# Queries of head pairs by seven block products in place of eight

## The chip, the cores and the metric

The kernel runs on one core of a Trainium2 chip. The metric is the device time of one execution in microseconds; less is better. TensorE (PE) multiplies, VectorE (DVE) and ScalarE (ACT) work elementwise, GpSimd (POOL) has a few statistics at the start, and SyncE (SP) issues nearly all DMAs.

## The reference

A layer norm feeds an attention block with cached keys and values (32 heads, 2048 queries, 2048 keys, head width 128) and a gated mixer (two residual blocks). The mixer's result, through SiLU, multiplies the attention's.

```python
xn = _layernorm(x)                                   # x: 2048 x 512
q = (xn @ wq).reshape(1, 2048, 32, 128)              # wq: 512 x 4096
p = softmax(einsum("bhqd,bhkd->bhqk", q, k_cache) * 128**-0.5)
s = einsum("bhqk,bhkd->bhqd", p, v_cache) @ wo       # wo: 4096 x 512
g = silu(mixer(xn, w1, w2, w3, w4))
return x + s * g
```

The change concerns `xn @ wq`.

## The kernel before, in words

After some 120 us of layer norms and mixer, the kernel walks through 128 *units*. A unit is one head with 512 queries: 8 groups of 4 heads, in each group 4 query quarters (`qt`), in each the 4 heads (`hh`). `HG` = 4, `NG` = 8, `QT` = 4, `NU` = 128, `SPU` = 8.

A unit has 8 *slots* (`p` = 0 to 7; `n` = 8 u + p counts them through). In each slot PE makes the scores of 256 keys (`s_slot`: two matmuls 128x512 into one of two score buffers) and the values of the slot ten before (`pv_run`: two matmuls 128x512). ACT takes the exponential of the scores, 128x1024, into `pT`. Beside that, most slots hold one more matmul, a filler: in slots 7, 0, 1, 2 the queries of the next unit (`q_mm`, four contraction chunks of 128, into `ps_q`, tag `xa`, one buffer), in slots 3 to 6 one token tile of the output projection (`wo_slot`, four heads, into `ps_wo`, tag `xm`, one buffer).

DVE does, in each unit and in this order: `turned_sums` of the unit before last (L383, L385), `add_next` (L345), `fold` (L349), `fold_last` (L353), `q_copy` of the next unit's queries (L318), `add_first` (L340), `add_next` (L345), `wo_post` (L467; more in the last groups), `norm` (L403). L340 and L345 add `pT` tiles into `acc` and wait for ACT. The row sums are turned by a DMA (`tT`), inverted, written out (`dr`) and read back to all partitions (`rb`), and `norm` multiplies the values with them.

In the last groups `wo_post` has more to do. In units 95 to 110 one `y_scale` (L433) or `y_add` (L438) comes in a unit, placed by `at`. For the later two query quarters of group 6 (posts in units 110 to 117) it is L460 and L463. For the first two quarters of group 7 (posts in units 118 to 125) it is L467, L476 and L478 and the output's DMA.

Every engine issues its instructions in the program's order. `pin` keeps the order in which the Python code emits them; `at(n, fn)` puts work at the end of slot n. A pool with n buffers makes the n+1st tile wait until the first is free. The last unit is cut into two token halves by hand-written code behind the loop.

Of the kernel before, what the change touches and what calls it, by code (L numbers as in the profile page):

```python
# [9 lines left out]
ALU = mybir.AluOpType  # L10
# [7 lines left out]
def kernel(  # L18
# [15 lines left out]
    nc = tc.nc  # L34
# [72 lines left out]
    w2_v = B_w2.rearrange("(dc p) j -> p dc j", p=P)  # L107
    w3_v = B_w3.rearrange("(dc p) f -> p dc f", p=P)

    def mm(out, lhsT, rhs, start, stop):  # L110
        pin(nc.tensor.matmul(out=out, lhsT=lhsT, rhs=rhs, start=start, stop=stop))  # L111

    pin(nc.vector.memset(warm[:], 0.0))
    pin(nc.vector.memset(ones_t[:], 1.0))
# [48 lines left out]
    vX = {}  # L163
    xin = {}

    def load_x(t, eng):
        xin[t] = tokp.tile([P, D], BF16, tag="ta", bufs=10, name="xin")
        pin(eng.dma_start(out=xin[t][:], in_=xsrc[t]))

    def load_pair(t, eng):  # L170
# [99 lines left out]
    def ln2(t):  # L270
        c, ts = divmod(t, 4)
        if ts == 0:
            xn2T[c] = pL.tile([P, DC, 512], BF16, tag="xn2T", bufs=2, name="xn2T")
        y = tokp.tile([P, D], BF16, tag="ta", bufs=10, name="xn2")
# [19 lines left out]
        pin(nc.vector.tensor_tensor(out=xall[:, t, :], in0=ps[:], in1=xall[:, t, :], op=ALU.add))  # L294

    def gate_tanh(t):
        th = tokp.tile([P, D], BF16, tag="ta", bufs=10, name="th")
        pin(nc.scalar.activation(out=th[:], in_=xall[:, t, :], func=ACT.Tanh, scale=0.5))
        return th

# [6 lines left out]
    def q_mm(u, dcs, tag="xa"):  # L307
        g, qt, hh = units[u]
        if dcs[0] == 0:
            st[u] = dict(psq=psX.tile([P, 512], FP32, tag=tag, name="ps_q"))  # L310
        for dc in dcs:
            mm(st[u]["psq"][:], wqs[g * HG + hh][:, dc, :],
               xnT[:, dc, qt * 512:(qt + 1) * 512], dc == 0, dc == DC - 1)

    def q_copy(u, eng=None):
        qT = qtp.tile([P, 512], BF16, name="qT")
        if eng is None:
            pin(nc.vector.tensor_copy(out=qT[:], in_=st[u].pop("psq")[:]))  # L318
        else:
            pin(nc.scalar.activation(out=qT[:], in_=st[u].pop("psq")[:], func=ACT.Identity))  # L320
        st[u]["qT"] = qT

    def s_slot(u, p):
        g, qt, hh = units[u]
# [126 lines left out]
    def wo_post(g, t, n):  # L451
        ps = wo_box.pop(0)
        if g == 0:
            sacc[t] = pS.tile([P, D], FP32, tag="sacc", bufs=NT, name="sacc")
            pin(nc.vector.tensor_copy(out=sacc[t][:], in_=ps[:]))
            return
        sa, gl = sacc[t][:], xall[:, t, :]
        if t // 4 in LATE and g >= GY:
            tm = pS.tile([P, D], FP32, tag="tm", bufs=4, name="tm")
            pin(nc.vector.scalar_tensor_tensor(  # L460
                out=tm[:], in0=ps[:], scalar=0.5, in1=gl, op0=ALU.mult, op1=ALU.mult))
            if g < NG - 1:
# [4 lines left out]
        pin(nc.vector.tensor_tensor(out=sa, in0=ps[:], in1=sa, op=ALU.add))  # L467
# [8 lines left out]
        pin(nc.vector.scalar_tensor_tensor(  # L476
            out=gl, in0=sa, scalar=0.5, in1=gl, op0=ALU.mult, op1=ALU.mult))
        pin(nc.vector.tensor_tensor(out=xl[:], in0=gl, in1=xl[:], op=ALU.add))  # L478
        pin(nc.sync.dma_start(out=out2d[t * P:(t + 1) * P, :], in_=xl[:]))
# [57 lines left out]
                   hh == 0, hh == HG - 1 and (ts in apart or c.stop == D))  # L537

    def last_act(ts, cols):
        tb[ts, cols.start] = tokp.tile([P, D // 2], BF16, tag="ta", bufs=10, name="tb")  # L540
# [241 lines left out]
    def wo_slot(part, n, each=2, **kw):  # L782
# [9 lines left out]
    q_plan = defaultdict(list)  # L792
    for v in range(1, NU):
        if v not in made:
            for dc in range(DC):
                q_plan[(v - 1) * SPU + dc - 1].append((v, (dc,)))

    for n in range(UB * SPU):
        u, p = divmod(n, SPU)
# [4 lines left out]
        pv_run(n)  # L804
        for v, dcs in q_plan.get(n, ()):
            q_mm(v, dcs)
        if p == 0 and u - 2 in TURN:
            turned_sums(u - 2)
        if p == 1 and u - 2 in TURN:
# [9 lines left out]
            twice = extra  # L819
        if twice and p < 3:  # L820
            wo_slot(p, n, tag="xa")
        if p == 3 and u + 1 not in made:
            q_copy(u + 1)
# [14 lines left out]
        if wo_p <= p <= wo_p + HG // each and wo_todo and pS is not None and (p == wo_p or wo_box):  # L838
            wo_slot(p - wo_p, n, each=each)
        if p == norm_p and u - 2 in TURN:  # L840
            norm_queue(u - 2)
        if p == 4:
            add_first(u)
        if p == 6:
# [19 lines left out]

    def last_stt(ts, cols):
        w = cols.stop - cols.start
        tb[ts, cols.start] = pS.tile([P, w], FP32, tag="tm", bufs=4, name="tm")
        pin(nc.vector.scalar_tensor_tensor(  # L868
            out=tb[ts, cols.start][:], in0=last_ps(ts, cols), scalar=0.5, in1=xall[:, t0 + ts, cols],
            op0=ALU.mult, op1=ALU.mult))  # L870

    def last_add(ts, cols, tm):
        if cols.start == 0:
            yl[ts] = tokp.tile([P, D], BF16, tag="ta", bufs=10, name="y")
        pin(nc.vector.tensor_tensor(out=yl[ts][:, cols], in0=tm, in1=sacc[t0 + ts][:, cols], op=ALU.add))  # L875

    def last_out(ts, cols, queue=nc.sync):
# [135 lines left out]
```

## Time and profile before

| | |
|---|---|
| median of 3 runs | 1243.86 us (1243.78 to 1243.9) |
| span of the profiled execution, first to last instruction | 1242.0 us |
| granted TensorE clock, mean | 1.000 |
| PE busy | 1231.2 us |
| ACT busy | 1110.7 us |
| DVE busy | 1006.7 us |
| mean of a 128x512 query copy (L318) | 683 ns |

The profiled execution's own time is its span; the runs' times lie 1.86 us above it by their median. In rows of a timeline stand the start, the time from start to shown end, engine, line, operation, output and inputs with shapes, how many in a row, and in brackets the idle time ahead with what ended it. A matmul's shown end lies behind the end of its stream, so that consecutive matmuls overlap in the rows; the rate is read from the starts. In a row of stretches come, after the window and its length, the busy time of PE, PEld (weight loads), DVE, ACT and POOL with their counts, then the granted clock, the share of DMA and GB/s.

### The profile page before, as it was taken

To read this page: it belongs to the slowest core of one execution; us is meant where nothing else is said; L and a number is where in the kernel's file an instruction comes from. 1 tells how busy PE (TensorE), PEld (TensorE's weight loads), DVE (VectorE), ACT (ScalarE), POOL (GpSimd) and SP (SyncE) were. 2 spreads that over 40 slices of the span, in tenths; PEclk is the share of its full clock that TensorE was granted. 3 is DMA by queue.
4 is the path that set the end of the run, shared out by engine and by line. 5 is a ranking of instruction groups with operands and counts; after the bars stand their busy time and mean duration, and the time that the engine had idled before them with its cause. 6 is when DMAs were issued, how large, how long until landed. Compare 5 with 4: busy or idle time off the path is not lost.

```text
span 1242.0 us, 16355 instructions
## 1 busy us (share of the span) xinstructions
PE 1231.2 (99%) x5822; PEld 613.6 (49%) x5937; DVE 1006.7 (81%) x1465; ACT 1110.7 (89%) x1127; POOL 26.6 (2%) x75
## 2 busy tenths in 40 slices
PE   9999999999999999999999999999999999999998
PEld 6444444444444444444444444444444444444445
DVE  7712778888888888888888888888888988999997
ACT  6345999999999999999999999999999999999996
POOL 5200000000000000000000000000000000000000
PEclk9999999999999999999999999999999999999999
DMA  7660113553335513453244423543346424552332
GB/s 180 165 141 29 30 39 75 92 110 73 68 80 104 111 40 85 89 112 77 56 103 90 103 53 72 104 104 69 73 85 113 101 60 89 99 109 63 77 79 66
DMA packets 244050, 107.67 MB, mean 87 GB/s; under 512 B 194816, under 2 KB 227712, under 8 KB 243968
## 3 DMA queue, kind: packets, MB, share of 16 engines
q1 hardware_dynamic: 243408, 106.17, 40.7%
q8 instruction: 46, 0.75, 0.3%
q10 hardware_dynamic: 560, 0.46, 0.1%
q14 instruction: 36, 0.29, 0.1%
HBM read 67.50 MB, written 2.36 MB: 56 GB/s over the span
## 4 chain that ended last, share of the span: by engine, by line
PE 98%; issue 1%; DMA 0%; DVE 0%; ACT 0%; POOL 0%; DVEq 0%
PE ps_s L111 42%; PE ps_o L111 38%; PE ps_q L111 8%; PE ps_wo L111 8%; PE ps_m L111 2%; DMA xin<-in_A_x_dram 0%; PE ps_oh L111 0%; DVE y L875 0%; DMA out_dram<-y 0%; DVE tm L868 0%; DVE tb L546 0%; ACT dump L202 0%; POOL rs L186 0%; PE ps_w L111 0%; DVE xall L217 0%
## 5 line engine op out<-in xcount | busy, mean ns | idle before, releaser
L334 ACT ACTIVATE pT<-ps_s 128x1024 bf16<-128x1024 f32 x1016 | 1038.1, 1024 | 59.4 <-PE ps_s L111 6.5
L111 PE MATMUL ps_s<-qT,kT 128*128 128x512 bf16 (+1 forms) x2061 | 608.5, 377 | 5.1
L111 PE MATMUL ps_o<-pT,vb 128*128 128x512 bf16 x1980 | 589.0, 379 | 0.2
L345 DVE TENSOR_TENSOR acc<-acc,pT 128x2048 bf16<-128x2048 bf16 x254 | 307.4, 1210 | 104.7 <-ACT pT L334 104.6
L111 PEld LDWEIGHTS <-kT 128*128 128x128 bf16 x2064 | 233.7, 113 | 217.7
L111 PEld LDWEIGHTS <-vb 128*128 128x128 bf16 x1984 | 194.0, 98 | 217.0
L340 DVE TENSOR_TENSOR acc<-pT 128x2048 bf16<-128x2048 bf16 x127 | 155.2, 1222 | 39.9 <-ACT pT L334 39.8
L111 PE MATMUL ps_wo<-wo_h,oT 128*128 128x512 bf16 x448 | 168.3, 379 | 0.1
L111 PE MATMUL ps_q<-xnT,wq_h 128*128 128x512 bf16 x458 | 167.4, 379 | 0.2
L349 DVE TENSOR_TENSOR acc<-acc 128x1024 bf16<-128x1024 bf16 x127 | 87.8, 691 | 4.3
L111 PEld LDWEIGHTS <-oT 128*128 128x128 bf16 x528 | 59.4, 113 | 57.8
L403 DVE TENSOR_TENSOR oT<-ps_o,rb 128x512 bf16<-128x512 f32 x127 | 86.6, 682 | 0.9 <-DMA rb<-dr 0.6
L383 DVE TENSOR_REDUCE sm<-tT 128x4 f32<-128x512 bf16 x124 | 83.9, 676 | 0.4 <-DMA tT<-acc 0.4
L318 DVE CAST qT<-ps_q 128x512 bf16<-128x512 f32 x116 | 79.3, 683 | 0.0
L111 PEld LDWEIGHTS <-wq_h 128*128 128x128 bf16 x508 | 49.7, 98 | 59.3
L467 DVE TENSOR_TENSOR sacc<-ps_wo,sacc 128x512 f32<-128x512 f32 x96 | 65.6, 683 | 0.0
L353 DVE TENSOR_TENSOR acc<-acc 128x512 bf16<-128x512 bf16 x127 | 54.1, 426 | 4.3
L285 ACT ACTIVATE h2T<-ps_s 128x1024 bf16<-128x1024 f32 x28 | 28.7, 1024 | 26.0 <-PE ps_s L111 25.3
L111 PE MATMUL ps_s<-xn2T,w_sb 128*128 128x512 bf16 x220 | 48.6, 379 | 0.2
L111 PEld LDWEIGHTS <-w_sb 128*128 128x128 bf16 x368 | 33.6, 98 | 29.6
L111 PEld LDWEIGHTS <-h2T 128*128 128x128 bf16 x224 | 21.9, 98 | 26.3
L294 DVE TENSOR_TENSOR xall<-ps_o,xall 128x512 bf16<-128x512 f32 x8 | 5.5, 692 | 36.0 <-PE ps_o L111 36.0
(86 smaller groups left out, 361.7 us busy)
## 6 DMA issues: line engine op xcount, KB each, us to landing
rb<-dr SPq DMA_DIRECT2D x127, 256.0 KB, 3.9
vb<-in_A_v_cache_dram SPq DMA_DIRECT2D x62, 256.0 KB, 3.0
wq_h<-in_A_wq_dram SPq DMA_DIRECT2D x32, 128.0 KB, 3.3
wo_h<-in_A_wo_dram SPq DMA_DIRECT2D x32, 128.0 KB, 3.0
w_sb<-in_B_w_dram SPq DMA_DIRECT2D x8, 256.0 KB, 4.8
kT<-in_A_k_cache_dram SPq DMA_TRANSPOSE x128, 2.8
xl<-in_A_x_dram SPq DMA_DIRECT2D x16, 128.0 KB, 3.2
dr<-rc SPq DMA_DIRECT2D x127, 2.0 KB, 1.4
```

Of the source, the lines that this page charges most:

```text
L111: pin(nc.tensor.matmul(out=out, lhsT=lhsT, rhs=rhs, start=start, stop=stop))
L285: pin(nc.scalar.activation(out=h2[c, f][:], in_=ps[:], func=ACT.Gelu_apprx_tanh))
L294: pin(nc.vector.tensor_tensor(out=xall[:, t, :], in0=ps[:], in1=xall[:, t, :], op=ALU.add))
L318: pin(nc.vector.tensor_copy(out=qT[:], in_=st[u].pop("psq")[:]))
L334: pin(nc.scalar.activation(out=s["pT"][-1][:, jj:jj + 2, :], in_=sps[:], func=ACT.Exp, scale=SCALE))
L340: pin(nc.vector.tensor_tensor(out=s["acc"][:], in0=s["pT"][0][:], in1=s["pT"][1][:], op=ALU.add))
L345: pin(nc.vector.tensor_tensor(out=a[:], in0=a[:], in1=st[u]["pT"][i][:], op=ALU.add))
L349: pin(nc.vector.tensor_tensor(out=a[:, 0:2, :], in0=a[:, 0:2, :], in1=a[:, 2:4, :], op=ALU.add))
L353: pin(nc.vector.tensor_tensor(out=a[:, 0, :], in0=a[:, 0, :], in1=a[:, 1, :], op=ALU.add))
L383: pin(nc.vector.tensor_reduce(out=sm[:], in_=s["tT"][:], axis=mybir.AxisListType.X, op=ALU.add))
L403: pin(nc.vector.tensor_tensor(out=to, in0=o, in1=rb, op=ALU.mult))
L467: pin(nc.vector.tensor_tensor(out=sa, in0=ps[:], in1=sa, op=ALU.add))
```

## The change

For 57 pairs of heads (units 12 to 125) the queries of two neighbouring heads and one query quarter are made together. The product has 512 tokens, 512 contraction rows and 2 x 128 output columns. It is cut in two along each: token halves, contraction halves, the two heads. Instead of eight block products, seven are formed from sums of blocks (the scheme of Strassen in Winograd's form). A block product is two matmuls 128x256, so a pair has 14 of them, where two units had eight of 128x512.

The sums of token blocks (`x_sum`, four for each query quarter, bf16, 128x512) and of weight blocks (`w_sum`, four for each pair of heads, bf16, 128x256) are made once, on DVE. The sums of products are made partly by PE, which adds two products in one half of a bank, and partly by DVE (`q_part`, four parts a pair, here q0 to q3) on the way from PSUM to the queries. Both halves, `ps[:, 0]` and `ps[:, 1]`, are one bank of tag `xa`.

For the pair (v, v+1), v even, everything happens two units ahead: products 1, 6, 2 in slots 1, 2, 5 of unit v-2 (the *even* unit), 7, 5, 4, 3 in slots 0, 1, 4, 5 of unit v-1 (the *odd* unit); q0 at slot 3 and q1 at slot 6 of the even unit, q2 at slot 3 and q3 at slot 6 of the odd one. On DVE q0 and q2 take the place of `q_copy`, ahead of `add_first`; q1 and q3 stand between `add_first` and `add_next`. q0 reads both halves (two operations), q1 copies one, q2 reads both (two operations, the second depends on the first), q3 is one operation of 128x512. The output projection's matmuls go to other slots (`at_wo`): 0, 3, 4, 6 or 3, 4, 5, 6 in even units, 0, 2, 3, 6 in odd ones, its post still at slot 7. The slots of a pair then hold 15 fillers instead of 16. The queries of unit 11 move four slots ahead, to slots 3 to 6 of unit 9.

To make room, small token tiles get other pools (`token`), the last head's values take a buffer of the common pool, early queries lie in the right-hand pool, and `tm` has two buffers. Behind the changed lines the numbers shift: `mm` is on L112, `q_part` on L388 to L400, `add_first` L422, `add_next` L427, `wo_post` L549, `norm` L485.

```diff
-    qtp = ent(pool("qt", 3 * HG + 2))
+    qtp = ent(pool("qt", 6))
+    qp2 = ent(pool("qp2", 2))
...
+    def x_sum(qt, i):
+        if i == 2 and qt < QT - 1:
+            out = x_block(qt, 1, LO)
+        else:
+            out = pS.tile([P, 2, 256], BF16, tag="xs", bufs=XS, name="xs")[:]
+        a, b, op = (
+            (x_block(qt, 1, LO), x_block(qt, 1, HI), ALU.add),
+            (xs.get((qt, 0)), x_block(qt, 0, LO), ALU.subtract),
+            (x_block(qt, 0, LO), x_block(qt, 1, LO), ALU.subtract),
+            (x_block(qt, 0, HI), xs.get((qt, 1)), ALU.subtract),
+        )[i]
+        pin(nc.vector.tensor_tensor(out=out, in0=a, in1=b, op=op))
+        xs[qt, i] = out
+
+    def w_sum(h, i):
+        if i == 0:
+            wc[h] = pS.tile([P, 4, 2, Dh], BF16, tag="wc", bufs=2, name="wc")
+        w, o = wc[h], [wc[h][:, k] for k in range(4)]
+        b11, b12, b21, b22 = (wqs[h + j][:, d, :] for d in (LO, HI) for j in (0, 1))
+        a, b = ((b12, b11), (b22, o[0]), (b22, b12), (b21, o[1]))[i]
+        pin(nc.vector.tensor_tensor(out=o[i], in0=a, in1=b, op=ALU.subtract))
+
+    def product(v, k):
...
+        if k in (1, 7):
+            s["ps"] = psX.tile([P, 2, 256], FP32, tag="xa", name="ps_q")
...
+        side, x, b = {
+            1: (0, x_block(qt, 0, LO), b11),
+            2: (0, x_block(qt, 0, HI), b21),
+            3: (1, xs[qt, 3], b22),
+            4: (0, x_block(qt, 1, HI), o[3]),
+            5: (1, xs[qt, 0], o[0]),
+            6: (1, xs[qt, 1], o[1]),
+            7: (0, xs[qt, 2], o[2]),
+        }[k]
+        for dc in range(2):
+            mm(s["ps"][:, side, :], b[:, dc, :], x[:, dc, :], k in (1, 7) and dc == 0, True, skip_group_check=True)
+
+    def q_part(v, i):
+        s = sw[v]
+        ps, t = s["ps"], lambda: pS.tile([P, 256], FP32, tag="tq", bufs=3, name="tq")
+        if i == 0:
+            m1, s["u"] = t(), t()
+            pin(nc.vector.tensor_copy(out=m1[:], in_=ps[:, 0, :]))
+            pin(nc.vector.tensor_tensor(out=s["u"][:], in0=ps[:, 1, :], in1=m1[:], op=ALU.add))
+        elif i == 1:
+            q = s["q"] = qp2.tile([P, 4, 256], BF16, name="qT")
+            pin(nc.vector.tensor_copy(out=q[:, 0, :], in_=ps[:, 0, :]))
...
+        elif i == 2:
+            u3 = t()
+            pin(nc.vector.tensor_tensor(out=u3[:], in0=ps[:, 0, :], in1=s["u"][:], op=ALU.add))
+            pin(nc.vector.tensor_tensor(out=s["q"][:, 3, :], in0=ps[:, 1, :], in1=u3[:], op=ALU.add))
+        else:
+            pin(nc.vector.tensor_tensor(
+                out=s["q"][:, 1:3, :], in0=ps[:], in1=s["u"][:].unsqueeze(1).to_broadcast([P, 2, 256]),
+                op=ALU.add))
...
-            tm = pS.tile([P, D], FP32, tag="tm", bufs=4, name="tm")
+            tm = pS.tile([P, D], FP32, tag="tm", bufs=2, name="tm")
...
+    FIRST, LAST = 12, NU - 4
+    pairs = range(FIRST, LAST + 1, 2)
     q_plan = defaultdict(list)
+    steps = defaultdict(list)
+    for v in pairs:
+        a = (v - 2) * SPU
+        for k, n in ((1, 1), (6, 2), (2, 5), (7, 8), (5, 9), (4, 12), (3, 13)):
+            steps[a + n].append((product, v, k))
+        for i, n in enumerate((3, 6, 11, 14)):
+            steps[a + n].append((q_part, v, i))
...
+    for qt, u in ((QT - 1, 8), (0, 10), (1, 14), (2, 18)):
+        for i in range(4):
+            at((u + i // 2) * SPU + 1 + 4 * (i % 2), lambda qt=qt, i=i: x_sum(qt, i))
+    for h in range(0, H, 2):
+        u = (h // HG) * QT * HG + (-4, -2)[h % HG // 2]
+        for i in range(4):
+            n = max(u, 8) * SPU if h < HG else (u + i // 2) * SPU
+            at(n + (2, 6)[i % 2] + (i // 2) * (h < HG) + 8 * (h % HG == 2) * (h < HG), lambda h=h, i=i: w_sum(h, i))
+
     for v in range(1, NU):
-        if v not in made:
+        if v not in made and not FIRST <= v < LAST + 2:
             for dc in range(DC):
-                q_plan[(v - 1) * SPU + dc - 1].append((v, (dc,)))
+                q_plan[(v - 1) * SPU + dc - 1 if v > FIRST else (v - 2) * SPU + dc + 3].append((v, (dc,)))
...
+        at_wo = [wo_p + i for i in range(HG // each + 1)]
+        if FIRST - 2 <= u < LAST:
+            at_wo = ([0, 3, 4, 6, 7], [0, 2, 3, 6, 7], [3, 4, 5, 6, 7], [0, 2, 3, 6, 7])[u % 4]
```

More of the change, by code (lines that the diff above doesn't have):

```diff
@@ L164, with token @@
     xin = {}
+    def token(early, name):
+        if early:
+            return pL.tile([P, D], BF16, tag="xi", bufs=5, name=name)
+        return tokp.tile([P, D], BF16, tag="ta", bufs=6, name=name)
     def load_x(t, eng):
-        xin[t] = tokp.tile([P, D], BF16, tag="ta", bufs=10, name="xin")
+        xin[t] = token(t < 5, "xin")
         pin(eng.dma_start(out=xin[t][:], in_=xsrc[t]))
@@ L321, in q_copy, with x_block @@
         st[u]["qT"] = qT
+    xs = {}
+    wc = {}
+    sw = {}
+    LO, HI = slice(0, 2), slice(2, 4)
+    def x_block(qt, half, dcs):
+        c = qt * 512 + 256 * half
+        return xnT[:, dcs, c:c + 256]
+    def x_sum(qt, i):
[11 more added lines that the diff above has]
+        xs[qt, i] = out
@@ new lines, in w_sum @@
+    def w_sum(h, i):
[6 more added lines that the diff above has]
+    def product(v, k):
+        g, qt, hh = units[v]
+        h = g * HG + hh
+        s = sw.setdefault(v, {})
+        if k in (1, 7):
+            s["ps"] = psX.tile([P, 2, 256], FP32, tag="xa", name="ps_q")
+        w, o = wc[h], [wc[h][:, i] for i in range(4)]
+        b11, _, b21, b22 = (wqs[h + j][:, d, :] for d in (LO, HI) for j in (0, 1))
+        side, x, b = {
[9 more added lines that the diff above has]
+            mm(s["ps"][:, side, :], b[:, dc, :], x[:, dc, :], k in (1, 7) and dc == 0, True, skip_group_check=True)
@@ new lines, in q_part @@
+    def q_part(v, i):
[8 more added lines that the diff above has]
+            pin(nc.vector.tensor_copy(out=q[:, 0, :], in_=ps[:, 0, :]))
+            for j in range(2):
+                st[v + j] = dict(qT=q[:, 2 * j:2 * j + 2, :].rearrange("d a b -> d (a b)"))
+        elif i == 2:
[6 more added lines that the diff above has]
+                op=ALU.add))
+            del sw[v]
@@ L806 @@
             q_mm(v, dcs)
+        run_steps(n, product)
         if p == 0 and u - 2 in TURN:
@@ L821 @@
             wo_slot(p, n, tag="xa")
-        if p == 3 and u + 1 not in made:
-            q_copy(u + 1)
+        for v, k in ((u + 1, 3), (u + 2, 7)):
+            if p == k and "psq" in st.get(v, ()) and (k == 3) == (v > FIRST):
+                q_copy(v)
+        if p == 3:
+            run_steps(n, q_part)
         if u - 2 in TURN:
@@ L837 @@
                 fold_last(u - 1)
-        if wo_p <= p <= wo_p + HG // each and wo_todo and pS is not None and (p == wo_p or wo_box):
-            wo_slot(p - wo_p, n, each=each)
+        if p in at_wo and wo_todo and pS is not None and (p == at_wo[0] or wo_box):
+            wo_slot(at_wo.index(p), n, each=each)
         if p == norm_p and u - 2 in TURN:
             norm_queue(u - 2)
+        if p != 3:
+            run_steps(n, q_part)
         if p == 4:
```

33 lines of the change are left out of this document (20 added, 13 removed).

## The prediction

> **What bounds the kernel now.** I read the page's busy line first, then the chain that ended last, then the engines in stretches of the span, and last the timelines of VectorE (DVE) and TensorE (PE) in single units.
>
> ```profile
> span 1242.0 us, 16355 instructions
> PE 1231.2 (99%) x5822; PEld 613.6 (49%) x5937; DVE 1006.7 (81%) x1465; ACT 1110.7 (89%) x1127; POOL 26.6 (2%) x75
> PE 98%; issue 1%; DMA 0%; DVE 0%; ACT 0%; POOL 0%; DVEq 0%
> 614.00:752.00 138.00, 137.37 (x629) 67.57 (x640) 116.03 (x160) 130.88 (x129) 0.00 (x0) 1.00 0.41 85
> 1028.00:1097.00 69.00, 68.68 (x316) 33.74 (x321) 62.14 (x89) 65.44 (x65) 0.00 (x0) 1.00 0.46 94
> 1097.00:1166.00 69.00, 68.63 (x314) 33.77 (x320) 63.12 (x92) 65.44 (x65) 0.00 (x0) 1.00 0.41 83
> 1166.00:1224.00 58.00, 57.74 (x278) 29.24 (x282) 55.46 (x80) 54.49 (x55) 0.00 (x0) 1.00 0.33 75
> ```
>
> The chain is PE for 98% of the span at a granted clock of 1.00: every matmul column removed shortens the time, as long as nothing else becomes late. The stretches show what could. DVE is busy 116.03 of 138 us (84%) in the middle, 90% from 1028, 91% from 1097 and 96% from 1166 us on. The change takes from PE and gives to DVE.
>
> **What PE gains.** A 128x512 and a 128x256 matmul stream at these rates:
>
> ```profile
> 16.95 3.49 PE ps_s L111 x32
> 45.52 4.32 PE ps_s L111 x20
> 16.79 3.66 PE L111 MATMUL ps_s<-xnT,w_sb 128*128 128x256 bf16 x32
> 606.60 0.59 PE L111 MATMUL ps_s<-qT,kT 128*128 128x512 bf16 x2
> 607.03 0.59 PE L111 MATMUL ps_o<-pT,vb 128*128 128x512 bf16 x2
> 607.46 0.38 PE L111 MATMUL ps_q<-xnT,wq_h 128*128 128x512 bf16 x1
> 607.67 0.59 PE L111 MATMUL ps_s<-qT,kT 128*128 128x512 bf16 x2
> ```
>
> 4.32/20 = 0.216 us for 512 columns, 3.49/32 = 0.109 us for 256, each with its own weight load, so the 14 loads a pair that replace 8 stay hidden. A pair of units needed 8 x 0.216 = 1.728 us of query matmuls and needs 14 x 0.109 = 1.527 us: 0.20 us a pair, 57 pairs, **11.4 us**. A slot holds two score and two value matmuls and one filler: 606.60 to 607.67, 1.08 us; without filler 0.86, with two 1.29. A pair of units is 16 slots, 17.27 us before and 17.07 after.
>
> ACT is no new bound. It needs one activation a slot, and where it lags it starts one every (124.43 - 120.47)/4 = 0.99 us, below the new mean slot of 1.067:
>
> ```profile
> 120.47 4.06 ACT L334 ACTIVATE pT<-ps_s 128x1024 bf16<-128x1024 f32 x4
> 124.43 0.62 ACT L298 ACTIVATE th<-xall 128x512 bf16<-128x512 bf16 x1
> ```
>
> **What DVE pays.** One unit of the last group, a whole period from one L345 to the next, with the 256-wide forms from the tail and the two waits of a middle unit below it:
>
> ```profile
> 1167.29 1.23 DVE L345 TENSOR_TENSOR acc<-acc,pT 128x2048 bf16<-128x2048 bf16 x1 [0.19 <-ACT pT L334]
> 1168.43 0.68 DVE L467 TENSOR_TENSOR sacc<-ps_wo,sacc 128x512 f32<-128x512 f32 x1
> 1169.15 0.69 DVE L476 SCALAR_TENSOR_TENSOR xall<-sacc,xall 128x512 bf16<-128x512 f32 x1
> 1169.88 0.42 DVE L478 TENSOR_TENSOR xl<-xall,xl 128x512 bf16<-128x512 bf16 x1
> 1170.22 0.68 DVE L403 TENSOR_TENSOR oT<-ps_o,rb 128x512 bf16<-128x512 f32 x1
> 1170.82 0.68 DVE L383 TENSOR_REDUCE sm<-tT 128x4 f32<-128x512 bf16 x1
> 1171.53 0.18 DVE L385 RECIPROCAL rc<-sm 128x4 f32<-128x4 f32 x1
> 1171.63 1.20 DVE L345 TENSOR_TENSOR acc<-acc,pT 128x2048 bf16<-128x2048 bf16 x1
> 1172.86 0.69 DVE L349 TENSOR_TENSOR acc<-acc 128x1024 bf16<-128x1024 bf16 x1
> 1173.58 0.42 DVE L353 TENSOR_TENSOR acc<-acc 128x512 bf16<-128x512 bf16 x1
> 1173.92 0.68 DVE L318 CAST qT<-ps_q 128x512 bf16<-128x512 f32 x1
> 1174.52 1.21 DVE L340 TENSOR_TENSOR acc<-pT 128x2048 bf16<-128x2048 bf16 x1
> 1175.92 1.23 DVE L345 TENSOR_TENSOR acc<-acc,pT 128x2048 bf16<-128x2048 bf16 x1 [0.19 <-ACT pT L334]
> 1234.19 0.42 DVE L868 SCALAR_TENSOR_TENSOR tm<-ps_w,xall 128x256 f32<-128x256 f32 x1 [1.10 <-PE ps_w L111]
> 1234.65 0.42 DVE L875 TENSOR_TENSOR y<-tm,sacc 128x256 bf16<-128x256 f32 x1
> L546 DVE TENSOR_TENSOR tb<-tb,xall 128x256 bf16<-128x256 bf16 x5 | 1.3, 284 | 0.0
> 603.97 1.23 DVE L340 TENSOR_TENSOR acc<-pT 128x2048 bf16<-128x2048 bf16 x1 [0.35 <-ACT pT L334]
> 606.13 1.23 DVE L345 TENSOR_TENSOR acc<-acc,pT 128x2048 bf16<-128x2048 bf16 x1 [0.93 <-ACT pT L334]
> ```
>
> An independent operation starts 0.08 us before the one ahead of it is shown to end (L403 to L383: 0.60 for 0.68); one that reads the result ahead starts 0.04 after its end (L467 to L476: 0.72; L868 to L875: 0.46). So a 512-wide PSUM operation costs 0.60 and a 256-wide one 0.34, or 0.46 when the next depends on it. Per pair q0 and q2 cost 0.46 + 0.34 each, q1 0.34, q3 0.60: 2.54. The two copies of L318 that go cost 1.20. **DVE gains 1.34 us of work a pair**, plus 64 weight sums of 0.20 (L546's 0.28 less 0.08) and 16 token sums of 0.34 (L353's 0.42 less 0.08). The Trainium skill would have this a little dearer: "VectorE: DVE Perf Modes", section "The DRAIN you can't avoid", says that a semaphore between two operations costs nothing extra, the next waits for the pipe either way. The rows differ (0.60 against 0.72), and the measurement decides; by the page the pair would gain 0.1 more.
>
> DVE's own work in a unit is the 8.63 us period less the waits, less 0.08 for each wait. Middle: 8.63 - 0.35 - 0.93 - 0.17 = 7.18. The units in which L433 or L438 runs (95 to 110):
>
> ```profile
> 951.46 1.23 DVE L345 TENSOR_TENSOR acc<-acc,pT 128x2048 bf16<-128x2048 bf16 x1 [0.77 <-ACT pT L334]
> 1089.59 1.23 DVE L345 TENSOR_TENSOR acc<-acc,pT 128x2048 bf16<-128x2048 bf16 x1 [0.64 <-ACT pT L334]
> ```
>
> 7.78. Those with L460 and L463 (110 to 117, the second row): 7.91. Those with L476 and L478 (from 118): 8.36. A pair after the change: 15.70, 16.90, 17.16, 18.06, against PE's 17.07.
>
> **Which wait ends last.** In the built program's order the first matmul of product 2 waits for q0, that of 7 for q1, that of 4 for q2, and the scores of the new unit for q3; behind each of them stand all later scores and values, and ACT behind those. I place a middle pair, even unit from 0, odd unit from 8.42. Data reach DVE 0.20 after a product's stream (L868 starts 0.04 after the end shown, which is 0.16 after the stream). q1 waits for product 2 (slot 5 ends 6.48) and runs 6.68 to 7.02; then L345 from 7.09, when its activation is done, for 1.14; L467 and L403 at 0.60 each, L383 0.71, L385 0.10, L345 1.23, L349 0.73, L353 0.34: 12.5. q2 is done at 13.4. Product 4 stands at 8.42 + 1.29 + 3 x 1.08 + 0.86 = 13.8. **Slack: about 0.4 us**; the others have more (q0 0.8, q3 1.0). In the middle the 39 pairs fit, and PE keeps its gain.
>
> When DVE is late at q2, a loop costs it time as well: product 4 starts 0.13 after q2's last slot (0.08, and 0.05 as in the two rows below), then 0.22 + 0.86 + 0.22 until product 3 is through, 0.20 to DVE: q3 can start 1.63 after q2, and DVE has only L340's 1.14 to do. 0.49 idle in every late pair.
>
> ```profile
> 5.12 0.35 DVE L211 TENSOR_SCALAR xall<-xin,mv,rs 128x256 bf16<-128x256 bf16 x1
> 5.52 0.10 PEld L111 LDWEIGHTS <-xall 128*128 128x128 bf16 x1 [0.39 <-DVE xall L211]
> ```
>
> Losses of PE: units 95 to 110, 8 pairs x (16.90 + 0.49 - 17.07) = 2.6; units 110 to 117, 4 x 0.58 = 2.3; units 118 to 123, 3 x 1.48 = 4.4; the 8 weight sums in units 108 to 111, 1.6. In the early part units 14 and 15 carry four token and four weight sums, 2.16: 15.70 + 2.16 + 0.49 - 17.07 - 0.4 = 0.9; units 18 and 19 0.1. In unit 9 the queries of unit 11 now stand four slots earlier, behind an evacuation on the same bank that DVE reaches after a token sum: about 0.7. Weight sums elsewhere: 0.1 a group, 0.6. Together **13.2 us**. The moved output matmuls (wo) keep their count; their new first place, slot 0 of every fourth unit, stands at 17.07 + 0.86 = 17.9 of a pair, and L467 frees its bank at 17.8 (q3 from 15.3, L345 behind it): covered by 0.1 while DVE is on time. Startup, tail and the DMA queue keep their instructions and order: nothing. A gain or loss of 0.5 there isn't excluded: of the 7.1 us from L385 to the L403 of the next period, the two transfers between them take 5.3, and more where the queue is busy.
>
> ```profile
> rb<-dr SPq DMA_DIRECT2D x127, 256.0 KB, 3.9
> dr<-rc SPq DMA_DIRECT2D x127, 2.0 KB, 1.4
> ```
>
> Sum: 1242.0 - 11.4 + 13.2 = 1243.8 for the span. The runs' median, 1243.86, lies 1.86 above the profiled span; with the same distance **1245.6 us**.
>
> The bank rule bears on this: the Trainium skill, "PSUM — Partial Sum Buffer", section "PSUM bank collisions raise a hardware error", wants PSUM guarded by bank and not by address, so product 4 has to wait for both reads of q2 although they are of two halves. The trace of before cannot show it; a guard by half would free product 4 0.34 earlier.
>
> **Rivals.** *PE keeps the gain* (chance 0.25). If the loop's idle time is filled, or the waits pass quicker than I put them, DVE loses only its plain excess: 3 x 0.99 + 4 x 0.09 + 8 x 0 + about 1.6 + 1.0 = 5.9, so about 1243.86 - 11.4 + 5.9 = 1238.4. For it: the middle has slack everywhere. Against: PE and DVE both issue in order, and product 3 stands a slot behind product 4.
>
> *The middle stalls too* (0.2). The slack at product 4 is 0.4 of a 17 us pair. If the 256-wide operations with an fp32 intermediate, which no row of before shows in this form, cost 0.1 more each, or rb is late by 0.5, all 39 middle pairs lose some 0.2 and the 15 late ones 0.3 to 0.6: 1245.6 + 8 + 9 at the worst, and with a third of that, the likelier size, 1251. It decides from 0.4 us a pair on. For it: in the late stretch DVE is already 96% busy. Against: L868 and L875 are nearly these operations.
>
> *The products don't stream at 0.109* (0.05), because weights come from three tiles in turn; from 1.728/14 = 0.123 on the gain is gone, and with the stalls the time is 1257. The 32 matmuls above speak against it.
>
> **How the numbers follow.** The forecast has 0.5; its own range, from a quicker or slower hand-over of 0.1 us at each stall and 1 us for startup and tail, is 1242 to 1249. To hold 8 in 10 the range reaches into the first two rivals: 1238 to 1251.5. The measurement tells from no change about 0.2%, 2.5 us: 1241.4 to 1246.4. Faster: the first rival, 0.25. Within: some three quarters of the forecast and a little of the second rival, 0.40. Slower: the rest, 0.35.
>
> **What would show it.** Right: PE busy falls by about 11 us, and its idle time grows from 11 to about 24, with ps_q on L112 waiting for DVE, nearly all of it after 940 us, at the first matmul of product 4; DVE shows waits for ps_q ahead of q1 and q3; DVE over 92% in the middle, about 98% from 1028 on. Wrong: ps_q stalls between 230 and 900 us (the second rival), no PE waits at the end (the first), or ps_q starts more than 0.11 us apart with nothing waited for (the third).

## The result, and the profile after

The changed kernel took **1248.65 us** (median of five runs, 1248.4 to 1249.49) against 1243.8 us for the kernel before (five runs, 1243.74 to 1243.9): ratio 1.0039, 95% interval 1.0026 to 1.0052. It is slower by 4.9 us, about twice what the measurement can tell from no change. The forecast was 1245.6, its range 1238 to 1251.5. The time lies in that range, but it is slower, to which the prediction gave 0.35, and not within what counts as no change, to which it gave 0.40.

The busy line, the chain's shares by engine, and the stretches of the kernel after; the columns are those of the lines before.

```profile
span 1246.5 us, 17349 instructions
PE 1224.5 (98%) x6159; PEld 645.3 (52%) x6279; DVE 1091.5 (88%) x1773; ACT 1092.7 (88%) x1127; POOL 26.8 (2%) x75
PE 73%; DVE 21%; issue 2%; DMA 2%; ACT 1%; SPq 0%; DVEq 0%; ACTq 0%
614.00:752.00 138.00, 137.27 (x682) 72.76 (x694) 128.52 (x202) 129.90 (x130) 0.00 (x0) 1.00 0.43 87
1028.00:1097.00 69.00, 66.51 (x328) 34.79 (x333) 66.00 (x110) 62.13 (x63) 0.00 (x0) 1.00 0.42 89
1097.00:1166.00 69.00, 66.47 (x329) 35.04 (x335) 65.99 (x104) 62.32 (x63) 0.00 (x0) 1.00 0.39 81
1166.00:1224.00 58.00, 55.42 (x269) 28.11 (x272) 55.81 (x87) 51.59 (x53) 0.00 (x0) 1.00 0.31 74
```

The span grew by 4.5 us. The chain was PE for 98%; now PE has 73% and DVE 21%. In the middle PE is as full as it was (137.27 of 138, before 137.37), at 93% of DVE. In the three late stretches PE has 2.5 to 2.6 us of idle time each, where before it had 0.3 to 0.4, and DVE is busy 96% of each.

Next, who waited for whom: after the engine, the line and the releaser come us in total, times, and the longest wait. The first six lines are of the whole span of after; behind them stand two of 240 to 932 us, and three of 932 us to the end.

```profile
ACT pT L416 <- PE ps_s L112: 45.9, 133, 1.5
DVE qT L400 <- PE ps_q L112: 26.0, 54, 0.5
DVE acc L422 <- ACT pT L416: 17.0, 32, 2.3
PE ps_q L112 <- DVE qT L398: 9.2, 15, 1.1
DVE acc L427 <- ACT pT L416: 6.7, 8, 1.6
DVE sm L465 <- DMA tT<-acc: 1.9, 6, 0.6
...
PEld L112 <- issue: 3.9, 16, 0.8
PE ps_q L112 <- DVE qT L398: 1.0, 2, 0.5
...
PEld L112 <- issue: 14.5, 22, 1.4
PE ps_q L112 <- DVE qT L398: 7.9, 12, 1.1
...
DVE oT L485 <- DMA rb<-dr: 0.7, 2, 0.4
```

PE waits for L398, the last operation of q2, mostly late in the span: 12 of 15 times and 7.9 of 9.2 us from 932 us on. PE's own list misses 120 matmuls (6159 beside 6279 weight loads), so that some of these waits probably stand as "issue" of a weight load. For the same reason the totals of busy PE, before (5822 of 5937) and after, can't be subtracted; I go by the *period of a pair* instead: the distance between the first score activations of two even units that follow each other. A row is named by the even unit in which the period starts, so the products in it are those of the pair two units later. Before, a period is 17.27 us from unit 10 on (17.24 in the last). After:

| pairs, by their even unit | period, us | lost against 17.07 |
|---|---|---|
| 8 (no pair product; 16.84 before) | 18.81 | 1.97 against 16.84 |
| 10, 12, 14, 16, 18 | 17.54, 17.10, 17.97, 17.14, 17.16 | 1.6 |
| 20 to 92, 37 pairs | 17.07, but 17.10 to 17.14 at weight sums and once 17.64 | 1.1 |
| 94 to 108 | 17.36 to 18.03 | 4.5 |
| 110 to 116 | 18.30, 17.82, 17.63, 17.62 | 3.1 |
| 118, 120, 122 | 18.08, 18.53, 18.53 | 3.9 |

57 pairs at 0.20 gained 11.4 us, and 16.2 were lost; 0.3 came back at units 124 and 125. So the span is 1242.0 - 11.4 + 16.2 - 0.3 = 1246.5 us, as measured. One late pair, in the timelines of DVE and PE:

```profile
1175.74 0.69 DVE L431 TENSOR_TENSOR acc<-acc 128x1024 bf16<-128x1024 bf16 x1
1176.46 0.42 DVE L435 TENSOR_TENSOR acc<-acc 128x512 bf16<-128x512 bf16 x1
1176.81 0.41 DVE L397 TENSOR_TENSOR tq<-ps_q,tq 128x256 f32<-128x256 f32 x1
1177.26 0.42 DVE L398 TENSOR_TENSOR qT<-ps_q,tq 128x256 bf16<-128x256 f32 x1
1177.60 1.22 DVE L422 TENSOR_TENSOR acc<-pT 128x2048 bf16<-128x2048 bf16 x1
1179.23 0.69 DVE L400 TENSOR_TENSOR qT<-ps_q,tq 128x512 bf16<-128x512 f32 x1 [0.42 <-PE ps_q L112]
1179.84 1.22 DVE L427 TENSOR_TENSOR acc<-acc,pT 128x2048 bf16<-128x2048 bf16 x1
...
1177.73 0.38 PE L112 MATMUL ps_q<-xnT,wc 128*128 128x256 bf16 x2 [1.14 <-DVE qT L398]
```

DVE does not stop until q2 is done at 1177.68. Only then can product 4 start (1177.73), while PE stood for 1.14 us. Product 3 comes a slot later, so DVE, which is the late engine, waits 0.42 us for it ahead of q3: both engines idle in one pair, in turn.

### The profile page after: what moved, and what is told of

The parts are those of the page before. It is cut to its first block, busy times and chain, and to the rows that moved or that the text cites. A ratio compares the mean times of both kernels' runs of the same rounds, so it can differ in the third digit from the quotient of the medians.

```text
span 1246.5 us, 17349 instructions
## 1 busy us (share of the span) xinstructions
PE 1224.5 (98%) x6159; PEld 645.3 (52%) x6279; DVE 1091.5 (88%) x1773; ACT 1092.7 (88%) x1127; POOL 26.8 (2%) x75
## 4 chain that ended last, share of the span: by engine, by line
PE 73%; DVE 21%; issue 2%; DMA 2%; ACT 1%; SPq 0%; DVEq 0%; ACTq 0%
PE ps_s L112 30%; PE ps_o L112 28%; PE ps_q L112 7%; DVE acc L427 6%; PE ps_wo L112 6%; PE ps_m L112 2%; DVE acc L431 2%; DVE sm L465 2%; DVE oT L485 2%; DVE acc L422 1%; DVE acc L435 1%; DVE sacc L549 1%; DMA rb<-dr 1%; DMA tT<-acc 1%; ACT pT L416 1%
## 5 line engine op out<-in xcount | busy, mean ns | idle before, releaser
L416 ACT ACTIVATE pT<-ps_s 128x1024 bf16<-128x1024 f32 x1016 | 1020.2, 1023 | 81.8 <-PE ps_s L112 45.9
L112 PE MATMUL ps_s<-qT,kT 128*128 128x512 bf16 (+1 forms) x2018 | 599.4, 377 | 0.7
L112 PE MATMUL ps_o<-pT,vb 128*128 128x512 bf16 x1936 | 579.8, 379 | 3.7
L427 DVE TENSOR_TENSOR acc<-acc,pT 128x2048 bf16<-128x2048 bf16 x254 | 306.6, 1207 | 7.1 <-ACT pT L416 6.7
L112 PEld LDWEIGHTS <-kT 128*128 128x128 bf16 x2064 | 232.9, 113 | 144.3 <-issue 1.4
L112 PEld LDWEIGHTS <-vb 128*128 128x128 bf16 x1984 | 193.8, 98 | 216.9 <-issue 0.3
L112 PE MATMUL ps_wo<-wo_h,oT 128*128 128x512 bf16 x484 | 181.9, 379 | 0.5
L422 DVE TENSOR_TENSOR acc<-pT 128x2048 bf16<-128x2048 bf16 x127 | 154.7, 1218 | 17.1 <-ACT pT L416 17.0
L485 DVE TENSOR_TENSOR oT<-ps_o,rb 128x512 bf16<-128x512 f32 x127 | 86.5, 681 | 1.0 <-DMA rb<-dr 0.7
L112 PEld LDWEIGHTS <-oT 128*128 128x128 bf16 x528 | 59.1, 113 | 49.9 <-issue 1.4
L112 PEld LDWEIGHTS <-wc 128*128 128x128 bf16 x456 | 44.5, 98 | 66.7 <-issue 16.0
L549 DVE TENSOR_TENSOR sacc<-ps_wo,sacc 128x512 f32<-128x512 f32 x96 | 65.6, 683 | 0.0
L112 PEld LDWEIGHTS <-wq_h 128*128 128x128 bf16 x394 | 38.5, 98 | 46.4 <-issue 0.9
L400 DVE TENSOR_TENSOR qT<-ps_q,tq 128x512 bf16<-128x512 f32 x57 | 39.4, 691 | 26.3 <-PE ps_q L112 26.0
L112 PE MATMUL ps_q<-xnT,wq_h 128*128 128x256 bf16 (+1 forms) x277 | 55.9, 291 | 1.6 <-DVE sacc L537 1.1
L112 PE MATMUL ps_q<-xs,wc 128*128 128x256 bf16 x258 | 49.3, 273 | 0.3
L112 PEld LDWEIGHTS <-w_sb 128*128 128x128 bf16 x368 | 33.5, 98 | 29.6
L112 PE MATMUL ps_s<-xn2T,w_sb 128*128 128x512 bf16 x220 | 48.6, 379 | 0.2
```

Of the source, the lines that this page charges most:

```text
L400: pin(nc.vector.tensor_tensor(out=s["q"][:, 1:3, :], in0=ps[:], in1=s["u"][:].unsqueeze(1).to_broadcast([P, 2, 256]), op=ALU.add))
L416: pin(nc.scalar.activation(out=s["pT"][-1][:, jj:jj + 2, :], in_=sps[:], func=ACT.Exp, scale=SCALE))
L422: pin(nc.vector.tensor_tensor(out=s["acc"][:], in0=s["pT"][0][:], in1=s["pT"][1][:], op=ALU.add))
L427: pin(nc.vector.tensor_tensor(out=a[:], in0=a[:], in1=st[u]["pT"][i][:], op=ALU.add))
L485: pin(nc.vector.tensor_tensor(out=to, in0=o, in1=rb, op=ALU.mult))
```

## The experiments

The theory: PE's gain is real; late in the span DVE has more than a pair's 17.07 us of work, and the loop from q2 over products 4 and 3 to q3 adds idle time to each late pair. Each edit below is against the changed kernel.

**e1_copies: the block sums of the products taken off DVE.** q0 and q2 are left out, q1 and q3 become plain copies, so the product sums aren't computed.

```diff
         if i == 0:
-            m1, s["u"] = t(), t()
-            pin(nc.vector.tensor_copy(out=m1[:], in_=ps[:, 0, :]))
-            pin(nc.vector.tensor_tensor(out=s["u"][:], in0=ps[:, 1, :], in1=m1[:], op=ALU.add))
+            pass
...
-            pin(nc.vector.tensor_copy(out=q[:, 0, :], in_=ps[:, 0, :]))
+            pin(nc.vector.tensor_copy(
+                out=q[:, 0:4:3, :], in_=ps[:, 0, :].unsqueeze(1).to_broadcast([P, 2, 256])))
...
+            pass
         else:
...
+            pin(nc.vector.tensor_copy(out=s["q"][:, 1:3, :], in_=ps[:]))
```

> The changed kernel with q0 and q2 left out and q1 and q3 as two plain copies of 128x512 out of PSUM, as many as before the change; the sums of products are thus not computed. Products, weight and token sums and the places of the output projection stay. Theory (the price of the change is DVE being late at q2, PE itself keeps its 11.4 us): PE stalls only in unit 9, about 1.1 us, and hardly after 940 us; time 1243.8 - 11.4 + 1.5 = about 1234, 1233 to 1236. Rival (the price lies on PE: products of 256 columns, weights out of three tiles, moved output matmuls, uneven slots that ACT can't follow): 1244 to 1248, since all of those stay.

Measured: 1234.98 us (1234.84 to 1235.04), ratio 0.9927 (0.9913 to 0.9942). The period is 17.07 in all but eight of the 57 pairs (seven with 17.14, one with 17.21), late ones too. Its busy line and the two late stretches:

```profile
span 1233.1 us, 17241 instructions
PE 1227.3 (100%) x6279; PEld 645.8 (52%) x6279; DVE 1025.4 (83%) x1545; ACT 1093.3 (89%) x1127; POOL 26.6 (2%) x75
1028.00:1097.00 69.00, 69.00 (x349) 36.35 (x348) 64.72 (x97) 64.97 (x65) 0.00 (x0) 1.00 0.46 100
1097.00:1166.00 69.00, 69.00 (x350) 36.44 (x348) 64.62 (x94) 64.99 (x66) 0.00 (x0) 1.00 0.39 79
```

PE is full. The seven products stream as they should; what the changed kernel loses beyond unit 8's 1.98 us and 0.6 elsewhere comes with the four parts on DVE. That ends the rival in which the products don't reach 0.109 us a matmul. Leaving q0 and q2 out takes away work of DVE and two hand-overs to PE at once; e3, e4 and e5 below tell these apart.

**e2_last92: pairs only up to units 92 and 93**, after them eight products by single heads; three token blocks that hold sums are rebuilt.

```diff
-    FIRST, LAST = 12, NU - 4
+    FIRST, LAST = 12, 92
...
-    for h in range(0, H, 2):
+    for h in range(0, 24, 2):
...
+    def x_back(qt):
+        b = x_block(qt, 1, LO)
+        pin(nc.vector.tensor_tensor(out=b, in0=x_block(qt, 0, LO), in1=b, op=ALU.subtract))
+
+    for qt in range(QT - 1):
+        at((LAST - 8 + 4 * qt) * SPU + 1, lambda qt=qt: x_back(qt))
```

> Pairs only up to units 92 and 93; groups 6 and 7 make their queries as before the change. Three token blocks that the sums had overwritten are rebuilt (3 operations of 0.34 us on DVE). Theory (the loss stands where DVE has its additional work, in units 94 to 123: 11.5 us by the pair periods of the two traces): 1248.65 - 11.5 + 15 pairs x 0.2 given back = 1240.2, 1239 to 1241.5, so faster than both. Rival (each pair costs the same, 4.8 us net over 57 pairs = 0.085 each): 1243.8 + 42 x 0.085 = 1247.4.

Measured: 1240.35 us (1239.77 to 1240.92), ratio 0.9971 (0.9959 to 0.9983). The periods from 94 to 122 are 17.27, as before the change. With 41 pairs instead of 57 the kernel is faster than either: the sixteen late pairs cost 11.5 us to gain 3.2, and the difference, 8.3, is what e2 saves.

**e3_p43: product 4 one slot later, beside product 3.** DVE's work stays.

```diff
-        for k, n in ((1, 1), (6, 2), (2, 5), (7, 8), (5, 9), (4, 12), (3, 13)):
+        for k, n in ((1, 1), (6, 2), (2, 5), (7, 8), (5, 9), (4, 13), (3, 13)):
```

> Product 4 moves one slot later, into slot 5 of the odd unit in front of product 3: both in one slot. Theory (a loop of q2, product 4, a slot, product 3, q3 leaves DVE idle for 0.49 us in each late pair, and the slack at product 4 is only 0.4): q3 can start 0.13 + 0.44 + 0.20 = 0.77 after q2, less than L340's 1.14, so no idle time; the slack at product 4 grows by 1.08 to about 1.5. Left is DVE's plain excess: 3 x 1.0 in units 118 to 123, 1.5 from the weight sums in 108 to 111, 0.3 between: 4.8 in place of 11.5 late, and units 14 and 15 nothing in place of 0.9: 1248.65 - 7.6 = 1241, 1239.5 to 1243. Rival (only DVE's sum of work counts, the loop fills itself): no change, 1248 to 1250, the longer slot 5 costing rather than helping.

Measured: 1240.57 us (1239.97 to 1240.86), ratio 0.9972 (0.9961 to 0.9983): 8.1 us less than the changed kernel. Two groups of waits of the whole span (the changed kernel has 26.0 us in 54 for the first, and 20.4 in 40 for the second), and then a late pair on DVE:

```profile
DVE qT L400 <- PE ps_q L112: 18.3, 37, 0.5
PEld L112 <- issue: 10.3, 27, 1.4
```

```profile
1152.17 0.42 DVE L398 TENSOR_TENSOR qT<-ps_q,tq 128x256 bf16<-128x256 f32 x1
1152.51 1.22 DVE L422 TENSOR_TENSOR acc<-pT 128x2048 bf16<-128x2048 bf16 x1
1153.64 0.68 DVE L400 TENSOR_TENSOR qT<-ps_q,tq 128x512 bf16<-128x512 f32 x1
1154.24 1.22 DVE L427 TENSOR_TENSOR acc<-acc,pT 128x2048 bf16<-128x2048 bf16 x1
```

L400 now follows L422 with no wait here, and PE's wait for L398 is down from 9.2 us in 15 places to 0.3 in one. Pairs 120 and 122 take 18.04 and 18.03, which is DVE's bare 18.06 of the prediction, where the changed kernel took 18.53; the pairs from 94 to 122 lose 4.1 us in place of 11.5. In sum these 7.4 us are 15 times the loop's 0.49, but pair by pair the saving lies between 0.07 and 0.86. At 110, 120 and 122, where DVE has more work than PE, it is 0.49 to 0.50. Pairs 94 to 108, whose DVE work lies just below 17.07, nearly fit now (17.07 to 17.29). Where a pair had lost more by other delays (96, 102, 108, 118), it saves 0.69 to 0.86, probably because product 4 now stands later and has more slack.

**e4_odd and e5_even: the same extra work in two places.** One reduction of 128x512 (0.60 us, its result unused) is added in slot 2 of every second unit from 20 to 91, in the odd units ahead of q2, or in the even units ahead of q0.

The edit of e4_odd is shown; e5_even has `u % 2 == 0`.

```diff
+        if p == 2 and 20 <= u < 92 and u % 2 == 1:
+            pin(nc.vector.tensor_reduce(out=sq[:], in_=sacc[0][:], axis=mybir.AxisListType.X, op=ALU.add))
```

> One more DVE operation of 0.60 us (a row sum of 128x512 fp32 that nobody uses) in slot 2 of each odd unit from 21 to 91, ahead of q2: 36 of them. Theory (what counts is the place: the slack at product 4 is 0.35 in every second pair and 0.57 in the others): losses of 0.25 and 0.03, up to 0.15 more each where DMA or the weight sums come on top: 36 x 0.14 = 5 to 8 us, 1254 to 1257, with stalls at the first matmul of product 4. Rival (DVE's share of busy time decides): 15.70 + 0.60 = 16.3 of 17.07 us, under 96%: no change, 1248.65, as with the same operation in even units.

> The same additional DVE operation of 0.60 us, 36 of them, now in slot 2 of each even unit from 20 to 90, ahead of q0 instead of q2. Theory: q1 stands behind it and waits for product 2 anyway; DVE's idle time there is 0.4 to 0.5 us, so q2 becomes late by 0.1 to 0.2 at most, less than the slack of 0.35 to 0.57 at product 4; product 2 has 0.8 of slack behind q0. Loss at most 0.1 in a pair and some more with weight sums: 1249 to 1252, against 1258.2 with the operation in odd units. Rival (DVE's sum of work in a pair decides, wherever it stands): the same time as with the odd units, 1258.

Measured: e4_odd 1258.21 us (1257.91 to 1261.32), ratio 1.012 (1.0105 to 1.0135); e5_even 1251.47 us (1250.9 to 1252.39), ratio 1.0061 (1.0048 to 1.0075). One stretch of the middle of after, e4_odd and e5_even, in this order:

```profile
300.00:640.00 340.00, 338.22 (x1680) 179.45 (x1713) 315.54 (x495) 319.82 (x320) 0.00 (x0) 1.00 0.40 82
```

```profile
300.00:640.00 340.00, 337.84 (x1693) 176.98 (x1691) 322.30 (x509) 316.13 (x316) 0.00 (x0) 1.00 0.39 80
```

```profile
300.00:640.00 340.00, 337.55 (x1672) 178.39 (x1704) 323.23 (x514) 318.13 (x318) 0.00 (x0) 1.00 0.39 80
```

DVE is equally busy (95%) in both, yet e4_odd adds 9.6 us to the changed kernel's median and e5_even 2.8. For e4_odd that is more than was expected (1254 to 1257): the pairs with further delays lost more than the 0.15 put for them. So the slack isn't one sum over the pair: it lies at places. Ahead of q0 the waits at q1 and q3 further on take up the 0.60 in plain pairs (17.07); ahead of q2 plain pairs alternate between 17.29 and 17.08, so the slack at product 4 is about 0.4 us in one and nearly 0.6 in the next. The plan of slots explains the difference: in even units divisible by 4 (36 and 40, say) an output matmul stands in slot 0, ahead of product 2, in the others (38 and 42) it doesn't. In the changed kernel's trace q1 (L392) starts 6.00 us behind the first activation of unit 36 and 5.78 behind that of unit 38, 0.22 apart, the time of one matmul of 512 columns, and q2 is as much later. In both kernels most pairs with weight sums, and a few others, lose more, mostly 0.3 to 0.6, at the worst 1.3 (pair 78 of e4_odd).

**e6_first20: pairs only from unit 20 on**, token and weight sums later, the first group by single heads.

```diff
-    FIRST, LAST = 12, NU - 4
+    FIRST, LAST = 20, NU - 4
...
-    for qt, u in ((QT - 1, 8), (0, 10), (1, 14), (2, 18)):
+    for qt, u in ((1, 14), (2, 18), (QT - 1, 22), (0, 26)):
...
-    for h in range(0, H, 2):
+    for h in range(HG, H, 2):
...
```

The queries made early are now those of unit 19, in slots 4 to 7 of unit 17, in place of those of unit 11 in unit 9.

> The first pair is at unit 20 in place of 12; the four token sums of a quarter are spread over units 14, 18, 22 and 26 on, the weight sums of group 0 go, and the queries that move ahead are those of unit 19 in place of unit 11. Theory: the early losses go (unit 9 about 1.3, pair 10 0.47, pair 14 0.9, others 0.2: 2.85 by the pair periods), four pairs give back 0.8: 1248.65 - 2.0 = 1246.6, 1245.8 to 1247.5. Rival (these losses belong to the start of the pairs and only move to units 17 to 22): 1248.65 + 0.8 = 1249.4.

Measured: 1248.28 us (1248.09 to 1249.18), ratio 1.0036 (1.0023 to 1.0049). My theory fell here. The period of units 8 and 9 is back at 16.84, and the period that now holds the early queries, at 16, takes 17.91, longer by no more than their three further matmuls (0.65): the loss of unit 9 is gone. But pairs 18, 26, 28, 32 and 40 now take 18.03, 17.43, 18.34, 17.80 and 17.40, 3.6 us over: these losses stand where the sums now are, instead of going away. The rival's 1249.4 is nearer than the theory's 1246.6, and neither is met. In pair 28 a transfer adds to them; DVE, late here already, waited for the turned row sums:

```profile
376.22 0.68 DVE L485 TENSOR_TENSOR oT<-ps_o,rb 128x512 bf16<-128x512 f32 x1
378.04 0.69 DVE L465 TENSOR_REDUCE sm<-tT 128x4 f32<-128x512 bf16 x1 [1.14 <-DMA tT<-acc]
```

**e7_best: the three cuts together**: e3's slot, pairs from 20 to 111, token blocks rebuilt at the end.

```diff
-    FIRST, LAST = 12, NU - 4
+    FIRST, LAST = 20, 110
...
-        for k, n in ((1, 1), (6, 2), (2, 5), (7, 8), (5, 9), (4, 12), (3, 13)):
+        for k, n in ((1, 1), (6, 2), (2, 5), (7, 8), (5, 9), (4, 13), (3, 13)):
...
-    for h in range(0, H, 2):
+    for h in range(HG, H - HG, 2):
...
```

> Three edits together: products 4 and 3 in one slot, the late start at unit 20, and pairs only to units 110 and 111, so that group 7 has no pairs and needs no weight sums; three token blocks rebuilt. 46 pairs. Theory: 46 x 0.2 = 9.2 gained; of the losses about 0.5 in the middle and 0.8 in units 94 to 109 stay (the pair periods with products 4 and 3 in one slot): 1243.9 - 9.2 + 1.3 = 1236, 1235 to 1237.5. Rival (the edits mend the same losses, so their gains don't add): no better than the best single one, 1240.

Measured: 1236.94 us (1236.56 to 1237.48), ratio 0.9944 (0.9932 to 0.9956). The gains add up, within the expected range; 46 pairs do better than 57.

**e8_places: e7_best with the sums in other slots**, out of the work ahead of q2 into places that the waits at q1 and q3 cover. Shown is what it has beyond e7_best.

```diff
-            at((u + i // 2) * SPU + 1 + 4 * (i % 2), lambda qt=qt, i=i: x_sum(qt, i))
+            w, p = ((u, 1), (u, 5), (u + 2, 1), (u + 2, 5))[i] if qt else ((u, 1), (u, 5), (u + 1, 5), (u + 1, 5))[i]
+            at(w * SPU + p, lambda qt=qt, i=i: x_sum(qt, i))
...
-            at(n + (2, 6)[i % 2] + (i // 2) * (h < HG) + 8 * (h % HG == 2) * (h < HG), lambda h=h, i=i: w_sum(h, i))
+            at(n + (2, 5, 5, 5)[i], lambda h=h, i=i: w_sum(h, i))
```

> e7_best with the token sums and the weight sums moved out of the slots whose VectorE work is on the path ahead of product 4 (slots 2, 6 and the token sums' slots 1 and 5 of one unit) into places that the waits ahead of q1 and q3 cover. Theory (the place of an added operation decides, as e4_odd and e5_even showed): this removes most of the about 1.1 us that the pairs at units 18, 20, 28 and 32 of e7_best still lose and the 0.07 us of each later group: 1236 us (1235.3 to 1236.7). Rival (the early remainders come from transposing transfers and row sums that land late beside the key loads, wherever the sums stand): 1236.9, as e7_best.

Measured: 1236.13 us (1235.4 to 1238.21), ratio 0.994 (0.9926 to 0.9953). The runs can't tell it from e7_best (their ranges overlap); the periods can: pairs 20, 28 and 32, which lost 0.21, 0.35 and 0.17 in e7_best, now lose 0.00, 0.03 and 0.00, and the later groups 0.00 in place of 0.07 (one keeps 0.10). Remainders stay: 0.12 each at 102 and 106, as in e7_best; 0.46 at 18, where DVE waits 0.96 us for the early queries (L327) and PE then waits for q0 behind a token sum; and a new 0.27 at 30, right behind a wait for turned sums that came late. SP's DMA issues there, and DVE's wait:

```profile
371.66 1.22 SPq L460 DMA_TRANSPOSE tT<-acc  x1
372.97 0.53 SPq L164 DMA_DIRECT2D wq_h<-in_A_wq_dram  x1
373.56 0.50 SPq L160 DMA_DIRECT2D vb<-in_A_v_cache_dram  x1
374.15 0.43 SPq L164 DMA_DIRECT2D wq_h<-in_A_wq_dram  x1
...
376.98 0.69 DVE L465 TENSOR_REDUCE sm<-tT 128x4 f32<-128x512 bf16 x1 [1.17 <-DMA tT<-acc]
```

So for the early pairs the place of the sums explains part of e6's losses, as shown here, and a late transfer stands beside another part; that it causes the 0.27, and the early queries the 0.46, is read from the order in the traces, not tested.

## Why the prediction was right, and where its sizes were off

- *PE gains 0.20 us a pair, 11.4 in all*: right. The period of the undisturbed pairs is 17.07, and e1_copies has it in all but eight pairs.
- *Durations on DVE*: right. The mean of a 256-wide operation with an fp32 intermediate is 417 to 424 ns, as the nearest rows said (0.42); dependent ones follow after 0.45 (1176.81 to 1177.26, forecast 0.46), independent ones after 0.34 (1177.26 to 1177.60). The section of the Trainium skill that the prediction sets against these rows ("VectorE: DVE Perf Modes", "The DRAIN you can't avoid") also says that a next operation that is not held starts earlier, so the 0.34 does not contradict that section as a whole; that a dependent operation costs 0.11 more here does differ from its sentence on the semaphore. The groups of the changed kernel, busy us and mean ns behind the bar, then idle time ahead:

```profile
L398 DVE TENSOR_TENSOR qT<-ps_q,tq 128x256 bf16<-128x256 f32 x57 | 24.2, 424 | 1.9
L397 DVE TENSOR_TENSOR tq<-ps_q,tq 128x256 f32<-128x256 f32 x57 | 23.7, 417 | 0.0
```

- *The place of the stall, product 4, behind both reads of q2*: right. Product 4, which writes the half that L397 reads, starts at 1177.73, behind L398, and not behind L397's end at 1177.22. The guard by bank that the Trainium skill wants ("PSUM — Partial Sum Buffer", section "PSUM bank collisions raise a hardware error") is what the trace shows, though bank and tile are one here and can't be told apart. What a guard by half would give wasn't tried; by these rows product 4 would be free 0.46 us earlier (1177.22 in place of 1177.68), not 0.34 as the prediction says, since the second read depends on the first.
- *The loop leaves DVE 0.49 idle in every late pair*: right. q3 starts 1.63 after q2's last slot as forecast (1177.60 to 1179.23), and L422 takes 1.14 of it. The row shows 0.42 because it counts from L422's shown end, 0.08 behind its slot. e3_p43 confirms it: with the loop gone, so is the wait. In the last two pairs 18.06 + 0.49 = 18.55 was forecast, 18.53 measured.
- *The middle keeps its gain with 0.4 us slack*: right in size (0.4 to 0.6 by e4_odd). 0.6 us of losses were forecast, 1.1 measured, and 0.57 of that in one pair (78), where DVE waited 0.58 us for turned sums. So the DMA queue's term, nothing with 0.5 not excluded, was put too low: the changed kernel waits for tT six times, 1.9 us, and late pairs 96 and 102, the two with 0.37 and 0.35 of waiting for the row sums that are read back (rb), lose 0.96 and 0.73 where their undisturbed neighbours lose 0.3. That a DVE without slack turns a late transfer into time fits all three, but no run delays a transfer by itself.
- *Late units 94 to 123, 10.9 us*: 11.5 measured. By parts, with the weight sums shared half and half: 3.4 forecast for 94 to 108 and 4.5 measured (most of the difference is pairs 96 and 102), for 110 to 117 3.1 and 3.1, for 118 to 123 4.4 and 3.9 (the first, 118, lost 1.0 and not 1.5). The close sum is partly luck, since the first and the last part err in opposite directions.
- *The early units, 1.7 us*: the step that was mis-sized most. 3.5 us were lost by the table, of which 0.65 is no loss: three query matmuls now stand in unit 9 instead of 10, and units 124 and 125 have three fewer (0.3 of it showed there). 2.9 remain. Unit 9's wait was found where forecast, but it held PE longer. DVE reached the evacuation L537 after its whole chain and a token sum, and PE waited with 1.10 us idle, where 0.7 was put:

```profile
206.15 0.42 DVE L352 TENSOR_TENSOR xs<-xnT 128x512 bf16<-128x512 bf16 x1
206.49 0.68 DVE L537 COPY sacc<-ps_wo 128x512 f32<-128x512 f32 x1
...
207.22 0.38 PE L112 MATMUL ps_q<-xnT,wq_h 128*128 128x512 bf16 x1 [1.10 <-DVE sacc L537]
```

  In e6_first20, where the early queries and the token sums stand elsewhere, this loss is gone; no run tells the two apart. The pair at 10 was not in the sum at all and lost 0.47; the pair at 14 was, with 0.9, and lost 0.90, that at 18 with 0.1, and lost 0.09.
- *The rivals*: "PE keeps the gain" fell, because the loop is real: without it, e3_p43 comes to 1240.6, near the 1238.4 of that rival; "the middle stalls too" fell, with 17.07 in the middle; the products' rate held (e1_copies). In sum 15.9 us were lost and not 13.2: the early units (1.2) and the middle with its late transfers (0.5) are 1.7 of the 2.7, the late part 0.6, the tail 0.3. The mechanism stood; the span came out at 1246.5 and not 1243.8. The forecast was a small difference of two terms of 11 and 13 us, so an error of a fifth in one of them turned "no change" into "slower".
- *What would show it*: idle time of PE was to grow from 11 to 24; the page has 22.0, with records missing. ps_q waits after 940 us: most of them, 12 of 15 from 932 us on. DVE over 92% in the middle: 93%. "About 98% from 1028" was too high: 96%, since DVE's rows show 0.42 us idle in each pair and 0.04 ahead of each dependent operation (1177.22 to 1177.26).

## What to carry to other kernels

Where two engines issue in order and hand tiles back and forth, don't ask for the free share of an engine but for its slack at each hand-over: 36 operations of 0.60 us more on DVE cost 10 us of the whole at one place and 3 at another. A saving on the bound engine that costs the next one work was worth having here only in the stages where that one had room: 41 of the 57 pairs, with nothing else changed, gave 0.9971 where all 57 gave 1.0039. When both engines wait in turn within one period, look for two hand-overs in a row that could be one; moving one product by a slot won 8 us.

## What the runs showed of the hardware

The transposing transfer of the row sums (`tT`) takes 3.8 us by its median from issue to landing, but single ones take much longer. The spread of before, then of after:

```profile
DMA to landing us min/median/max: 3.3/3.7/5.8
DMA to landing us min/median/max: 3.3/3.8/5.5
```

In e8_places the transfer issued at 371.66, with weight and value loads issued right behind it, landed at 376.96, after 5.30 us. Such loads don't explain the late ones, though: of the 124 transfers of that trace, 33 had a weight or value load issued within 2 us behind them, with a median of 3.9 us and 3 above 5 us; the other 91 had a median of 3.9 as well, and 8 above 5 us. What makes single ones late stays open.

The spread is no larger after the change than before it. The kernel before had waits of DVE for ACT that could take it up, 104.6 us at one line in its groups of waits; in the changed kernel the same wait (L427) is down to 6.7:

```profile
DVE acc L345 <- ACT pT L334: 104.6, 124, 1.3
```

In the changed kernel's trace 26 of the 37 pairs from 20 to 92 repeat to within 0.002 us, so that losses of 0.03 us a pair can be read from a single trace, far below what the runs' times resolve.
